# Batch 1's strided attention outputs: transposed by DMA through DRAM in place of TensorE

## The chip, the cores and the metric

The kernel runs on one core of one Trainium2 chip. The metric is device time in microseconds (us) of one execution, as a median over runs. Engines: PE is TensorE, DVE VectorE, ACT ScalarE, POOL GpSimd, SP SyncE, which only issues DMAs here. PEld in a profile is TensorE's weight loads, which overlap its matmuls.

## The reference

Sparse attention over 8 batches and 8 heads (576 positions, head size 64), then a bilinear feed-forward over all 4608 tokens:

```python
scores = scale * np.matmul(q, k.transpose(0, 1, 3, 2))
rel = pos[:, None] - pos[None, :]
mask_local = (rel >= 0) & (rel < stride)                 # stride 32
mask_strided = (rel >= 0) & (pos[None, :] % stride == pos[:, None] % stride)
masks = np.stack([mask_local if h < H // 2 else mask_strided for h in range(H)], axis=0)
...
attn_out = np.matmul(attn, v)                            # [8, 8, 576, 64]
x = attn_out.transpose(0, 2, 1, 3).reshape(B * S, H * D) # [4608, 512]
a = x @ w_a                                              # w_a, w_b: [512, 1536]
b = x @ w_b
return a * b @ w_out                                     # w_out: [1536, 512]
```

## The kernel before

**Tiling.** Attention is worked batch by batch, eight heads as four head pairs c = 0 to 3 (0 and 1 local, 2 and 3 strided) of two units each: u = 2c + half. The feed-forward is worked in nine tiles t of 512 tokens. Its input is `xT`, the attention output with features on the partitions and tokens along the row, one chunk of 128 features for each head pair; it is a ring of four batches (XR = 4). Batch 1 lies in columns 576 to 1151, of which tile 1 (tokens 512 to 1023) reads 576 to 1023 in all four chunks.

**An order written by hand.** All engines run their instructions in program order, which a table of slots sets. A tile has sixteen slots: twelve of `ffn_ab` (the products with w_a and w_b, L622) and four of `ffn_y` (the product with w_out, L872). Tile 0 is slots 0 to 15, tile 1 begins at slot 16. Positions such as 12.5 lie inside a slot. `STEPS[1]` (L580 to 582) lists what of batch 1's attention is issued at each position: T transposes q or k (`Tk`, `Tq`), S computes scores, exp and mask, V multiplies by the values and normalizes, X transposes a head pair's output into `xT`; L0 and L1 (`lead_vl`, L231) copy rows of `vl`, the local heads' values, on DVE; W0 to W3 (L175) make sums of `wo_sb`; D1 is the first step of batch 2's k. Slot 13 holds some(1) of six w_out matmuls, then position 12.5, three matmuls of each of the two token groups with 12.6 and 12.75 behind them, the last three of each, and position 13. The w_out matmuls at 6 to 8 and 9 to 11 of the second index read slices 2 and 3 of `wo_sb`, each loaded by its own DMA (L255).

**Outputs of batch 1.** V writes a normalized unit into `xn[1, z]` (a tile `xr`) with positions on the partitions; for the strided pairs (z = 1) that is 72 partitions by 8 positions by 4 heads by 64, position 8p + g on partition p. V5 completes pair 2, V7 completes pair 3. `step_X` (L564) then makes, for c >= 2, eight PE transposes of 72 by 128 into a `tp` bank (L550) and one ACT copy of 128 by 576 into `xT` (L562). X2 stands at position 12.75, X3 at 13, X0 at 14, X1 at 15.

**Values of batch 1.** V0, at position 13, is the first local unit of batch 1. It reads `vl_buf[1]`, which a GpSimd DMA loads (L225, issued behind the four DMAs of `wo_sb`), and whose first 32 partitions L0 copies from the others once the load has landed.

**The path through DRAM.** From batch 2 on the local pairs go another way: `rows_out` (O) writes a pair's outputs to a DRAM tile `xd`, as 576 rows of 128 numbers (144 KB), and `rows_in` (I) reads it back with a DMA transpose into `xT`. Both are issued on SP's queue in program order; the second waits on SP for the first to land. In `LATER` these are O0, I0, O1, and I1. Batches 0 and 1 do not use this path before the change.

**What tile 1 waits for.** At the first slot of tile 1 `ffn_ab` takes the chunks in the order 0, 2, 3 for w_a, then for w_b, and chunk 1 last (`late = 1`, L637), since X1 is the last step before.

**Loads.** GpSimd's queue issues all loads, with a conversion from float32 to bfloat16; in slots 0 and 1 the four `wo_sb` DMAs, `vl` of batch 1, and batch 2's k and q (L212, L203). SP's queue carries the results (L883 for tiles 0 and 1), batch 2's spread of k and q (L342, L346) and, from batch 2 on, O and I.

Of the kernel before, what the change touches and what calls it, by code (L numbers as in the profile page):

```python
# [17 lines left out]
NP = 72  # L18
# [3 lines left out]
LW = 96  # L22
# [9 lines left out]
def kernel(  # L32
# [10 lines left out]
    nc = tc.nc  # L43
    B, H, S, D = q.shape
# [392 lines left out]
    xn = {}  # L437
# [64 lines left out]
    scratch = {}  # L502

    def rows_out(b, c):

        scratch[b, c] = dram.tile([S, 2 * D], BF16, tag=f"xd{c}", name=f"xd{c}")
        nc.sync.dma_start(out=scratch[b, c].rearrange("(g p) (h d) -> p g h d", p=LW, d=D),
                          in_=xn[b, 0][:, :, 2 * c:2 * c + 2])

    def rows_in(b, c):  # L510

# [52 lines left out]
    def step_X(b, c):  # L564
# [12 lines left out]
        F1b F0c F1c""".split()  # L577


    STEPS = {1: {5.5: "Tk2", 6: "Tq2", 7: "S4 Tk3", 7.5: "S5", 8: "Tq3", 8.5: "V4", 9: "S6 V5 Pk0", 9.5: "S7 Pq0",  # L580
                 10: "V6 Tk0", 10.5: "Tq0 Pk1 Z0", 11: "Pq1", 12: "V7 Tk1 S0 W0 W1", 12.5: "Tq1 W2",
                 12.6: "S1", 12.75: "L0 X2", 13: "s2 X3 V0 m2 L1 W3", 13.5: "V1 S3", 14: "V2 X0", 14.5: "V3 D1", 15: "X1"},
             2: {20: "S0", 20.5: "S1", 21.5: "V0", 22: "S2", 23: "V1", 23.5: "S3", 24.5: "V2", 25: "S4", 26: "V3", 26.5: "S5",
                 27.5: "V4", 28: "S6", 28.5: "V5", 29: "S7", 29.5: "V6", 30.5: "V7"}}
    LATER = {-1: "S0", 0: "S1", 1: "V0", 2: "S2", 3: "V1 O0", 4: "S3", 5: "V2", 6: "S4 I0", 7: "V3 O1", 8: "S5", 9: "V4",
# [2 lines left out]
    IN_Y = {2: "S7", 6: "V6", 11: "V7"}  # L588
    FN = {"Tk": step_Tk, "Tq": step_Tq, "S": step_S, "V": step_V, "X": step_X, "W": lambda b, n: fast_w(n, slice(0, 3)),
          "s": S_px, "m": S_m, "L": lead_vl, "O": rows_out, "I": rows_in, "Pk": lambda b, c: pair_up("k", c), "Pq": lambda b, c: pair_up("q", c),  # L590
          "Z": lambda b, n: zero_qz(0, nc.vector, ((1, 1),)), "D": lambda b, n: step_D(FIRST_D, 0, "k", n)}

# [308 lines left out]
    with tc.manual_schedule(engines={ENG.PE, ENG.SP, ENG.Pool, ENG.DVE, ENG.Activation}):  # L901
# [11 lines left out]
        for x, src in ((raw[0], k), (raw[1], q)):  # L913
            nc.sync.dma_start(out=x[:96].rearrange("p (h r d) -> p h r d", h=2, d=D),
                              in_=src[0, 0:2].rearrange("h (p r) d -> p h r d", r=RL))
# [62 lines left out]
        for b in range(1, B):  # L978
            for pos, names in (STEPS.get(b) or {16 * (b - 1) + x: n for x, n in LATER.items()}).items():
                steps.setdefault(pos, []).append((b, names.split()))  # L980
            if b not in STEPS:
                for n, names in IN_Y.items():
# [104 lines left out]
```

## Time and profile before

| | us |
|---|---|
| median of 3 runs (lowest to highest) | 326.13 (326.02 to 326.52) |
| the profiled execution: its time | 326.3 |
| the profiled execution: its span in the trace | 324.6 |
| PE busy | 317.0 (98%) |
| DVE busy | 258.5 (80%) |
| ACT busy | 188.9 (58%) |
| POOL busy | 160.3 (49%) |
| packets of GpSimd's queue q0, share of 16 DMA engines over the span | 65.1% |
| packets of SP's queue q1, the same share | 25.3% |

The span runs from the first instruction to the last; 1.7 us of the profiled execution's time lie outside it. A busy share is a mean over stages: that PE is busy 98% of the span says that work taken from PE, or a wait put on it, shows in the time, if nothing else holds PE at that place. The DMA share can be above 100%, since packets of one engine overlap. The granted clock was 0.998 of full speed.

### The profile page before, as it was taken

How to read it: one execution, taken by the hardware profiler on the slowest of the kernel's cores; microseconds unless marked ns; L12 is line 12 of the kernel's file. 1: busy time of each engine (PE TensorE's matmuls, PEld its weight loads, DVE VectorE, ACT ScalarE, POOL GpSimd, SP SyncE). 2: the span in 40 equal slices, each digit the busy share in tenths (PEclk: the TensorE clock that was granted, in tenths of full speed). 3: DMA queues.
4: the chain of work that ended last, by engine and by line, in shares of the span. 5: the costliest groups of instructions: out<-in, count | busy, mean ns of one | idle time of the engine just before them, and what ended most of it. 6: DMA issues, size and time to landing. Idle time of an engine off the chain costs nothing.

```text
span 324.6 us, 7425 instructions
## 1 busy us (share of the span) xinstructions
PE 317.0 (98%) x2651; PEld 209.4 (65%) x2680; DVE 258.5 (80%) x559; ACT 188.9 (58%) x329; POOL 160.3 (49%) x289
## 2 busy tenths in 40 slices
PE   8999999999999999999999999999999999999994
PEld 7754555455555587557999885569455966686573
DVE  6767888888778899898889888988999768837842
ACT  6763775478764576447644764476546655335441
POOL 8945837699857554853576247644013012203300
PEclk9999999999999999999999999999999999999999
DMA  9999999899999999999999979999145040004004
GB/s 154 154 204 201 203 185 174 170 181 132 139 213 136 133 95 98 118 218 131 107 107 191 172 90 108 174 174 120 43 108 140 14 129 3 0 0 131 0 3 129
DMA packets 110724, 40.43 MB, mean 125 GB/s; under 512 B 88672, under 2 KB 107744, under 8 KB 110688
## 3 DMA queue, kind: packets, MB, share of 16 engines
q0 software_dynamic: 85968, 19.48, 65.1%
q1 hardware_dynamic: 24576, 20.42, 25.3%
q8 instruction: 21, 0.34, 0.5%
q14 instruction: 15, 0.12, 0.1%
q10 hardware_dynamic: 144, 0.07, 0.1%
HBM read 39.51 MB, written 10.91 MB: 155 GB/s over the span
## 4 chain that ended last, share of the span: by engine, by line
PE 88%; DMA 6%; POOL 2%; ACT 1%; DVE 1%; issue 1%; POOLq 0%
PE mm L622 46%; PE mm L808 14%; PE mm L872 6%; PE st L388 4%; PE mm L706 4%; PE o L466 2%; PE ax L699 2%; DMA xd<-xl 2%; PE o L525 2%; DMA xT<-xd 2%; DMA vl<-in_v_dram 2%; PE mm L699 2%; PE mm L837 2%; POOL shared L197 1%; PE end L837 1%; PE ab L622 1%
## 5 line engine op out<-in xcount | busy, mean ns | idle before, releaser
L622 PE MATMUL mm<-xT,wb_sb 128*128 128x512 bf16 (+1 forms) x404 | 93.3, 354 | 0.4
L622 PE MATMUL mm<-xT,wa_sb 128*128 128x512 bf16 (+1 forms) x391 | 92.1, 353 | 1.0 <-DMA xT<-xd 0.2
L643 ACT COPY a_sb<-mm 128x512 f32<-128x512 f32 x90 | 52.7, 586 | 53.8 <-PE mm L622 51.8
L622 PEld LDWEIGHTS <-wb_sb 128*128 128x128 bf16 x416 | 40.2, 98 | 36.6 <-DVE pf L711 0.4
L1053 POOL CAST pace<-pf 1x1 f32<-1x1 bf16 x83 | 24.9, 300 | 71.2 <-DVE pf L646 51.6
L646 DVE TENSOR_TENSOR pf<-a_sb,mm 128x512 bf16<-128x512 f32 x68 | 46.2, 680 | 9.6 <-PE mm L622 8.1
L622 PEld LDWEIGHTS <-wa_sb 128*128 128x128 bf16 x416 | 37.5, 98 | 24.4 <-issue 0.5
L409 ACT ACTIVATE p<-st 72x576 bf16<-72x576 f32 (+1 forms) x56 | 36.4, 650 | 14.4 <-PE st L388 14.2
L541 DVE TENSOR_TENSOR xT<-o,xr 64x288 bf16<-64x288 f32 x48 | 21.4, 446 | 14.8 <-ACT xr L535 14.3
L808 PEld LDWEIGHTS <-ps 128*128 128x128 bf16 x288 | 28.0, 98 | 3.1
L785 ACT COPY y_sb<-mm 128x512 f32<-128x512 f32 (+1 forms) x28 | 15.6, 556 | 17.9 <-PE mm L808 15.3
L808 PE MATMUL mm<-wf,ps 128*128 128x256 bf16 x216 | 25.5, 273 | 0.0
L534 ACT ACTIVATE xr<-o 64x576 f32<-64x576 f32 x28 | 18.1, 648 | 11.9 <-PE o L525 11.6
L872 PE MATMUL mm<-wo_sb,pf 128*128 128x512 bf16 x93 | 23.0, 379 | 0.2
L243 POOL DMA_DIRECT2D vs<-in_v_dram x24 | 19.6, 820 | 4.9 <-PE mm L808 2.4
L808 PEld LDWEIGHTS <-pf 128*128 128x128 bf16 x216 | 20.3, 98 | 2.6 <-issue 0.2
L1053 POOL COPY pace<-y_sb 1x1 f32<-1x1 f32 x23 | 5.2, 226 | 33.1 <-DVE y_sb L783 19.8
L535 ACT ACTIVATE xr<-xr 64x576 f32<-64x576 f32 x28 | 19.1, 683 | 0.9
L212 POOL DMA_DIRECT2D ql<-in_q_dram x24 | 16.0, 666 | 5.8 <-DMA wo_sb<-in_moe_w_out_dram 4.9
L808 PE MATMUL mm<-wo_sb,pf 128*128 128x256 bf16 x144 | 18.5, 273 | 0.1
L212 POOL DMA_DIRECT2D kl<-in_k_dram x24 | 16.1, 670 | 4.7 <-issue 3.9
L706 PE MATMUL mm<-xT,wb_sb 128*128 128x512 bf16 x60 | 18.3, 379 | 0.1
(189 smaller groups left out, 566.6 us busy)
## 6 DMA issues: line engine op xcount, KB each, us to landing
out_dram<-y_sb SPq DMA_DIRECT2D x12, 512.0 KB, 6.0
out_dram<-y_sb SPq DMA_DIRECT2D x11, 256.0 KB, 4.0
vl<-in_v_dram POOLq DMA_DIRECT2D x6, 384.0 KB, 8.2
kl<-in_k_dram POOLq DMA_DIRECT2D x24, 72.0 KB, 3.2
ql<-in_q_dram POOLq DMA_DIRECT2D x24, 72.0 KB, 3.4
vs<-in_v_dram POOLq DMA_DIRECT2D x24, 72.0 KB, 4.3
wo_sb<-in_moe_w_out_dram POOLq DMA_DIRECT2D x4, 384.0 KB, 9.7
natk<-in_k_dram POOLq DMA_DIRECT2D x20, 72.0 KB, 3.6
```

Source lines behind the costliest of these rows:

```text
L212: nc.gpsimd.dma_start(out=t[32 * h:32 * h + 32], in_=src[b, h].rearrange("(i y) d -> y i d", y=32))
L243: nc.gpsimd.dma_start(out=vs_buf[b % 2][:, h, :, 0:D], in_=v[b, HL + h].rearrange("(p r) d -> p r d", r=RS))
L409: nc.scalar.activation(p_flat(p)[:M, :2 * W].rearrange("p (i n) -> p i n", n=2 * n), st[:M].rearrange("p a (i n) -> p (a i) n", n=256)[:, ...
L535: nc.scalar.activation(r, r, ACT.Exp, scale=-1.0)
L541: nc.vector.tensor_mul(dst.rearrange("d (p r) -> d p r", r=RS)[:, :, G * half:G * (half + 1)], o[:64, j, :W].rearrange("d (g p) -> d p g", ...
L622: nc.tensor.matmul(ps_[:, c0:c0 + n], lhsT=w[:, kk, 128 * f:128 * (f + 1)], rhs=xT[:, kk, x0:x0 + n], start=(kk == first and c0 == 0), sto ...
L643: nc.scalar.copy(a_sb, ab[0])
L646: nc.vector.tensor_mul(pf[:, f, :].rearrange("p (i a s) -> p a i s", i=2, s=16), halves(a_sb), halves(ab[1]))
L706: nc.tensor.matmul(got[e], lhsT=wb_sb[:, kk, 128 * f:128 * (f + 1)], rhs=xT[:, kk, x0:x0 + TTOK], start=kk == 0, stop=kk == KD - 1)
L808: nc.tensor.matmul(bank[b][:, q], lhsT=lhs(g, q), rhs=rhs(g), start=k in "172" and q == 0 and g == 0, stop=g == FG - 1, skip_group_check=True)
L872: nc.tensor.matmul(ybank[j], lhsT=pf[:, f, 128 * j:128 * (j + 1)], rhs=wo_sb[:, f], start=(f == 0), stop=(f == FD - 1))
L1053: nc.gpsimd.tensor_copy(pace, done)
```

## The change

`rows_out` takes the strided pairs too: the DRAM tile's rows are then written as `(p g)`, 72 partitions by 8 rows, from `xn[b, 1]`. In the table of batch 1 the steps X2 (at 12.75) and X3 (at 13) go, and O2 comes behind V5 at slot 9, I2 behind V6 and Tk0 at slot 10, O3 behind V7 at slot 12, and I3 at 12.5 behind Tq1 and W2. X0 and X1 stay as they are. `rows_in` is unchanged.

```diff
     def rows_out(b, c):
 
         scratch[b, c] = dram.tile([S, 2 * D], BF16, tag=f"xd{c}", name=f"xd{c}")
-        nc.sync.dma_start(out=scratch[b, c].rearrange("(g p) (h d) -> p g h d", p=LW, d=D),
-                          in_=xn[b, 0][:, :, 2 * c:2 * c + 2])
+        order = dict(pattern="(g p) (h d) -> p g h d", p=LW) if c < 2 else dict(pattern="(p g) (h d) -> p g h d", p=NP)
+        nc.sync.dma_start(out=scratch[b, c].rearrange(order.pop("pattern"), d=D, **order),
+                          in_=xn[b, c // 2][:, :, 2 * (c % 2):2 * (c % 2) + 2])
...
-    STEPS = {1: {5.5: "Tk2", 6: "Tq2", 7: "S4 Tk3", 7.5: "S5", 8: "Tq3", 8.5: "V4", 9: "S6 V5 Pk0", 9.5: "S7 Pq0",
-                 10: "V6 Tk0", 10.5: "Tq0 Pk1 Z0", 11: "Pq1", 12: "V7 Tk1 S0 W0 W1", 12.5: "Tq1 W2",
-                 12.6: "S1", 12.75: "L0 X2", 13: "s2 X3 V0 m2 L1 W3", 13.5: "V1 S3", 14: "V2 X0", 14.5: "V3 D1", 15: "X1"},
+    STEPS = {1: {5.5: "Tk2", 6: "Tq2", 7: "S4 Tk3", 7.5: "S5", 8: "Tq3", 8.5: "V4", 9: "S6 V5 Pk0 O2", 9.5: "S7 Pq0",
+                 10: "V6 Tk0 I2", 10.5: "Tq0 Pk1 Z0", 11: "Pq1", 12: "V7 O3 Tk1 S0 W0 W1", 12.5: "Tq1 W2 I3",
+                 12.6: "S1", 12.75: "L0", 13: "s2 V0 m2 L1 W3", 13.5: "V1 S3", 14: "V2 X0", 14.5: "V3 D1", 15: "X1"},
```

## The prediction

> **What bounds the kernel now.** I read the page first (busy times), then TensorE's timeline around the two steps that go, then the timelines of VectorE and SyncE and the DMA issues of the same stretch, and last every DMA of the path through DRAM in the later batches.
>
> ```profile
> PE 317.0 (98%) x2651; PEld 209.4 (65%) x2680; DVE 258.5 (80%) x559; ACT 188.9 (58%) x329; POOL 160.3 (49%) x289
> ```
>
> PE is busy 98% of the span, so the whole kernel is bound by it; 16 transposes less should show, unless PE is held at this place by something else. TensorE's timeline there (start us, us, engine, line, what):
>
> ```profile
> 48.08 0.42 PE L550 MATMUL tp<-ident,xr 72*128 72x72 bf16 x8
> 48.34 1.46 PE L872 MATMUL mm<-wo_sb,pf 128*128 128x512 bf16 x5
> 49.64 0.41 PE L388 MATMUL st<-qz1l,kT1l 128*128 128x192 bf16 x3
> 49.89 0.42 PE L550 MATMUL tp<-ident,xr 72*128 72x72 bf16 x8
> 50.15 0.35 PE L466 MATMUL o<-vl,p 128*128 128x65 bf16 x6
> ...
> 56.87 0.81 PE L622 MATMUL mm<-xT,wa_sb 128*128 128x512 bf16 x3
> ```
>
> X2 starts at 48.08 and the next group at 48.34; X3 at 49.89, the next (V0) at 50.15. Each step takes 0.26 us of PE's order. Tile 1 begins at 56.87. What V0 needs is in VectorE's timeline, whose bracket gives the idle time before the row and what ended it, and in the DMA issues of 36.9 to 37 (KB and us to landing at the end):
>
> ```profile
> 49.73 0.35 DVE L231 COPY vl<-vl 32x704 bf16<-32x704 bf16 x1 [0.55 <-DMA vl<-in_v_dram]
> ```
>
> ```profile
> wo_sb<-in_moe_w_out_dram POOLq DMA_DIRECT2D x1, 384.0 KB, 11.9
> vl<-in_v_dram POOLq DMA_DIRECT2D x1, 288.0 KB, 12.8
> ```
>
> The load of `vl`, issued at 36.91, lands at 49.71. VectorE is waiting for it and copies until 50.08; V0 starts at 50.15. So V0 stands within 0.07 us of its data: X2 and X3 fill time that PE would otherwise wait. The loads before it are as tight: slice 3 of `wo_sb`, issued at 36.16, lands at 48.1, and the first matmul that reads it is in the row at 48.34. How full the DMA engines are is in the last two columns of the windows (DMA share, GB/s; the first is the stretch in us):
>
> ```profile
> 38.00:42.00 4.00, 4.00 (x48) 2.44 (x46) 3.78 (x11) 2.40 (x4) 2.69 (x5) 1.00 1.25 206
> 42.00:46.00 4.00, 3.94 (x37) 2.29 (x36) 3.43 (x9) 2.92 (x5) 0.82 (x2) 1.00 1.44 197
> 46.00:50.00 4.00, 3.95 (x38) 2.39 (x37) 2.68 (x6) 3.29 (x7) 1.33 (x3) 1.00 2.29 152
> 50.00:54.00 4.00, 4.00 (x48) 2.40 (x47) 3.32 (x10) 2.61 (x5) 4.00 (x8) 1.00 1.44 207
> ```
>
> Until 50 all of this is GpSimd's loads, with a share far over 1: they queue, and the landings above are 11.9 and 12.8 us after issue. PE is the bound by its busy time, but from 46 to 50 it walks just behind that queue.
>
> **What is removed.** Sixteen transposes, 2 x 0.26 = 0.52 us of PE, and two copies of 0.64 us on ACT. The copies lie off the path: ACT idles 0.75 us before the exp at 52.26. Without X2 and X3 PE comes to V0 at 50.15 - 0.52 = 49.63, but the copy of `vl` still ends at 50.08. Of the gain 50.15 - 50.08 = 0.07 us could be left; I take **0**. Behind V0 nothing changes for PE up to tile 1, and it shows no gap there to refill.
>
> **What is added, on SP.** SP's queue is empty from 15 to 49.80 (its first row there is the result store), so nothing holds O2. V5's last VectorE row is 0.69 us at 39.62: O2 issues at 40.4. The later batches show these operations so (SP's rows of 210 to 222, then of 242 to 256):
>
> ```profile
> L507 SPq DMA_DIRECT2D xd<-xl x1: 523/523/523, 215.5 to 215.5; - x1
> L512 SPq DMA_TRANSPOSE xT<-xd x2: 1148/1210/1271, 214.1 to 222.0; - x2
> DMA to landing us min/median/max: 6.1/6.5/7.0
> ```
>
> ```profile
> L507 SPq DMA_DIRECT2D xd<-xl x1: 534/534/534, 247.6 to 247.6; - x1
> L512 SPq DMA_TRANSPOSE xT<-xd x2: 1129/1142/1156, 246.3 to 250.0; - x2
> DMA to landing us min/median/max: 2.4/2.5/2.6
> ```
>
> With loads in flight (210 to 222, share 1.34) 6.1 to 7.0 us each, with none (246 on) 2.4 to 2.6. O2 alone in SP's queue beside loads is nearest to the write at 105.0, 3.4 us at a share of 0.9; at 1.25 to 1.44 I take 5.0 (bounds 3.4 and 6.5): it lands at 45.4. I2 issues then. O3 is queued behind it, and its data (VectorE's row of 0.69 us at 45.30) is there at 46.0. From the issue of a first transpose to the landing of the second, with a write queued between, the trace has 145.45 to 152.47 + 3.7 = 10.7 us, 179.88 to 190.5 = 10.7, 214.08 to 222.0 + 6.1 = 14.0 and, without loads, 246.35 to 252.6 = 6.2. With 10.7, I3 lands at **56.1**; at best O3 issues at 46.1 and I3 lands two transfers of 2.5 later, 51.1; at worst 46.9 + 14.0 = 60.9.
>
> PE wants I3's chunk as the third matmul of tile 1, 0.43 us into it: 57.30 now. So the middle case is in time. Behind I3 on SP wait the two stores of 49.80 and 50.45, whose buffer is needed again only in tile 1's `ffn_y` at 80 us, and batch 2's k at 57.07, behind I3's issue in every case but the last. No cost.
>
> **What is added, on the DMA engines.** Each of the four transfers moves 144 KB (147,456 bytes) on the engines that carry the loads. If the total rate stays, a transfer of SP's queue pushes the loads behind it by 147,456 bytes over the rate of the stretch: 0.72 us at 206 GB/s (O2, 41 to 45) and 0.97 us at 152 GB/s (I2, 45 to 50). Both are through before `vl`: **0.72 + 0.97 = 1.69 us later**, and O3 may add 0.97. The bounds: 0, if the loads keep their pace (50 to 54 moved 207 GB/s with the stores between, so 152 may not be a ceiling), and 2.66 with O3. I take 1.69, the two transfers that surely lie ahead of it. `wo_sb`'s slice 3 is late by part of the same, which is inside that and not added.
>
> The Trainium skill ("DMA: Bandwidth & Descriptors", section Queues, rings and completion order) says that each DMA engine alternates between the queues that have work, a whole packet at a time. By it the four transfers would not wait for the whole queue of loads, only share with it, and I3 would land near the early bound; the 256 KB store at 49.80, landed in 4.0 us while loads of 5 to 12 us were in flight, agrees. The sum stays 1.69, since by the rule the loads pay.
>
> A page that speaks against the change is "VectorE: DVE Perf Modes" (the Trainium skill, section Rules for kernel authors): transpose on TensorE where PSUM can take the result. The rows here, 0.26 us and a copy of 0.64 against two landings of 2.4 to 7.0, agree; it gives no other sum.
>
> **The sum.** V0 starts at 50.15 + 1.69 = 51.84, tile 1 at 58.56, and I3 (56.1) is there before 58.99. All behind moves with PE: with 98% busy no later gap takes 1.7 us back, and the loads after tile 0 are paced by GpSimd's copies of finished results. 326.3 + 1.69 - 0 = 328.0 for the profiled execution, which stands 0.17 above the median: **327.8**. By the bounds 0 and 2.66 it is 326.1 to 328.8.
>
> **Rivals.**
>
> *The transposed chunk comes late.* I3's landing takes the place of V0 as what holds PE, at the first slot of tile 1, from the point where it lands after 57.30 plus the loads' delay. At the slow bound 60.9 tile 1's third matmul is 3.6 us later than now: 329.7. For it: the share of 1.44 to 2.29 here is above that of the 14.0 us case. Against it: those landings had more of SP's own transfers between.
>
> *The loads keep their pace.* The engines take the 590 KB beside the loads, V0 stays pinned at 50.15, and nothing shows: 326.1. For it: the rate rose to 207 GB/s when stores came; against it: landings of 12 us show a queue that is full for 15 us.
>
> *Faster: V0 is not pinned.* The mechanism is at V0 too: it needs `vl` 0.5 us earlier than now. It decides if the load, bound by the order of packets and not by the engines, lands before 49.2; then the 0.52 us come through, 325.6, and with the two pauses before positions 42.3 and 48.8 in the chain of waits (0.06 and 0.05) 325.5. For it: `vl`'s landing is one execution's; against it: no edit hastens GpSimd's queue.
>
> **How the numbers follow.** My forecast gets 0.52, the late chunk 0.17, the loads at pace 0.18, V0 free 0.13. The predicted time is the first's, 327.8, its own range 326.8 (one transfer of 0.72) to 328.8. A measurement of this kernel can tell 0.2%, 0.65 us. Slower by more: the first and second, 0.69. Within: the third and some 0.05 of the fourth, 0.23. Faster by more: what is left of the fourth, 0.08, as its full 0.63 us just meets the bound. The range has to take in all but 0.2: from 325.8 (half of the gain) to 329.8 (the late chunk at its bound).
>
> **What would show it.** L550 with 40 transposes for 56, L562 with 6 copies; four more SP rows with `xd`. Right, if VectorE's row of L231 stands near 51.4 with a wait on `vl`, V0 near 51.8 and tile 1 near 58.6 with no wait on `xT`. The late chunk would show as a wait of L622 on the DMA `xT<-xd` near 58 to 61. The loads at pace: L231 at 49.7 still. Wrong altogether, if V0 starts before 50.0.

## The result and the profile after

The changed kernel takes 331.35 us (median of 5 runs, 331.14 to 332.76) against 326.52 us of the kernel before beside it: a ratio of 1.0163 (of the means; 95% interval 1.014 to 1.0185), 4.8 us slower by the medians. Forecast was 327.8, in a range that ended at 329.8. The direction was right, the size was not, and the mechanism was that of the first rival. Here are busy times and granted clock of the page:

```profile
span 329.5 us, 7426 instructions
PE 320.7 (97%) x2664; PEld 209.7 (64%) x2664; DVE 259.0 (79%) x559; ACT 187.9 (57%) x327; POOL 160.5 (49%) x289
PEclk9999999799999999999999999999999999999998
```

TensorE does 16 transposes less, but the two busy times (317.0 before, 320.7 after) don't compare: the page before has 2651 matmuls for 2680 weight loads, so its trace lacks some records, and the page after has 2664 for 2664. The clock row is the sign to go by: ahead of the run's end one slice in 40 has a lower granted clock, the one from 57.7 to 65.9 us. That is where tile 1 begins. TensorE's timeline there:

```profile
50.90 0.31 PE L466 MATMUL o<-vl,p 128*128 128x65 bf16 x5 [0.19 <-DVE vl L231]
...
57.58 0.60 PE L623 MATMUL mm<-xT,wa_sb 128*128 128x512 bf16 x2
61.13 0.38 PE L623 MATMUL mm<-xT,wa_sb 128*128 128x512 bf16 x1 [2.96 <-DMA xT<-xd]
61.35 1.36 PE L623 MATMUL mm<-xT,wb_sb 128*128 128x512 bf16 x3
...
63.36 1.78 PE L623 MATMUL mm<-xT,wa_sb 128*128 128x512 bf16 x4
```

Two matmuls of tile 1 run, on chunks 0 and 2. The third needs chunk 3, and TensorE stands still for 2.96 us until I3 has landed. What follows runs slowly: four matmuls take 1.78 us at 63.36, where the same group took 1.03 us before:

```profile
58.59 1.03 PE L622 MATMUL mm<-xT,wa_sb 128*128 128x512 bf16 x4
```

The windows (stretch; busy us of PE, PEld, DVE, ACT, POOL; granted clock; DMA share; GB/s) show why:

```profile
60.00:61.00 1.00, 0.00 (x0) 0.00 (x0) 0.00 (x0) 0.00 (x0) 0.96 (x1) 1.00 1.09 394
61.00:62.00 1.00, 0.86 (x3) 0.34 (x3) 0.00 (x0) 0.00 (x0) 0.17 (x1) 0.73 1.07 393
62.00:63.00 1.00, 1.00 (x4) 0.36 (x3) 0.00 (x0) 0.00 (x0) 0.00 (x0) 0.50 0.66 234
63.00:64.00 1.00, 1.00 (x4) 0.38 (x3) 0.20 (x1) 0.59 (x1) 0.00 (x0) 0.50 0.35 102
64.00:65.00 1.00, 1.00 (x4) 0.32 (x3) 1.00 (x2) 0.00 (x0) 0.17 (x1) 0.56 0.33 77
65.00:66.00 1.00, 1.00 (x6) 0.46 (x5) 0.97 (x3) 0.59 (x1) 0.90 (x1) 1.00 0.43 110
```

After the wait the granted clock is 0.50 for some 3.4 us (by what the windows from 61 to 65 lack to 1.00). SyncE's queue shows why I3 is late:

```profile
40.95 1.02 SPq L508 DMA_DIRECT2D xd<-xr  x1
48.86 1.23 SPq L513 DMA_TRANSPOSE xT<-xd  x1
50.13 0.85 SPq L508 DMA_DIRECT2D xd<-xr  x1
55.06 1.13 SPq L513 DMA_TRANSPOSE xT<-xd  x1
```

O2 is issued at 40.95, and I2, which waits for it to land, at 48.86: **7.9 us** for a write that took 2.4 to 7.0 us in the later batches. O3, whose data is there at 46.6, is behind I2 and goes out at 50.13; I3 follows at 55.06 (4.9 us) and lands 6.03 us later, at 61.09.

The loss, as places in the two traces. Third matmul of tile 1: 57.30 before, 61.13 after, so 3.8 us, of which 0.7 us had been there at V0 (50.15 and 50.90). By 66 us the same rows stand 5.5 us apart: the half clock adds 1.7 us. From 228 us on 5.1 us are left, and the spans differ by 4.9. V0's own start is set by the copy of `vl`, in VectorE's timeline:

```profile
50.50 0.35 DVE L231 COPY vl<-vl 32x704 bf16<-32x704 bf16 x1 [0.54 <-DMA vl<-in_v_dram]
```

It stands 0.77 us later than before, where the prediction had about 1.69. TensorE was 0.8 us late at 44 us already, before O2 had moved a packet, so this lateness is the execution's own. The two steps that are gone would have left 0.3 us of it at V0; the wait for `vl`, which landed 13.3 us after its issue in place of 12.8, made it 0.7 again.

### The profile page after: what moved, and what is told of

Read it like the earlier page. It is cut to its first block, busy times and chain, and to the rows that moved or that the text cites. A ratio compares the mean times of both kernels' runs of the same rounds, so it can differ in the third digit from the quotient of the medians.

```text
span 329.5 us, 7426 instructions
## 1 busy us (share of the span) xinstructions
PE 320.7 (97%) x2664; PEld 209.7 (64%) x2664; DVE 259.0 (79%) x559; ACT 187.9 (57%) x327; POOL 160.5 (49%) x289
## 4 chain that ended last, share of the span: by engine, by line
PE 83%; DMA 11%; POOL 2%; DVE 1%; ACT 1%; issue 0%
PE mm L623 41%; PE mm L809 17%; DMA shared<-in_k_dram 4%; PE mm L707 4%; DMA vl<-in_v_dram 4%; PE st L388 4%; PE mm L873 3%; PE misc L155 3%; PE o L526 2%; PE ax L700 2%; DMA xT<-xd 2%; PE mm L838 2%; PE mm L700 2%; DMA xd<-xr 1%; PE o L466 1%; PE end L838 1%
## 5 line engine op out<-in xcount | busy, mean ns | idle before, releaser
L623 PE MATMUL mm<-xT,wa_sb 128*128 128x512 bf16 (+1 forms) x408 | 94.9, 357 | 3.0 <-DMA xT<-xd 3.0
L623 PE MATMUL mm<-xT,wb_sb 128*128 128x512 bf16 (+1 forms) x408 | 94.5, 356 | 0.2 <-DMA wb_sb<-in_moe_w_b_dram 0.2
L647 DVE TENSOR_TENSOR pf<-a_sb,mm 128x512 bf16<-128x512 f32 x68 | 46.3, 680 | 9.2 <-PE mm L623 8.1
L786 ACT COPY y_sb<-mm 128x512 f32<-128x512 f32 (+1 forms) x28 | 15.6, 556 | 17.8 <-PE mm L809 14.5
L535 ACT ACTIVATE xr<-o 64x576 f32<-64x576 f32 x28 | 18.1, 648 | 11.9 <-PE o L526 11.6
L649 DVE TENSOR_TENSOR pf<-a_sb,mm 128x512 bf16<-128x512 f32 x22 | 14.9, 677 | 8.5 <-ACT a_sb L644 6.6
L707 PE MATMUL mm<-xT,wb_sb 128*128 128x512 bf16 x64 | 19.0, 379 | 0.0
```

Of the source, the lines that this page charges most:

```text
L535: nc.scalar.activation(r, sums, ACT.Ln)
L623: nc.tensor.matmul(ps_[:, c0:c0 + n], lhsT=w[:, kk, 128 * f:128 * (f + 1)], rhs=xT[:, kk, x0:x0 + n], start=(kk == first and c0 == 0), sto ...
L647: nc.vector.tensor_mul(pf[:, f, :].rearrange("p (i a s) -> p a i s", i=2, s=16), halves(a_sb), halves(ab[1]))
L707: nc.tensor.matmul(got[e], lhsT=wb_sb[:, kk, 128 * f:128 * (f + 1)], rhs=xT[:, kk, x0:x0 + TTOK], start=kk == 0, stop=kk == KD - 1)
```

## The experiments

Theory *late chunk*: the four DMAs wait for each other on SyncE's queue, I3 comes after TensorE asks for it, and TensorE's idling lowers its clock. Rival *loads pay*: what the prediction took for the likeliest, the added bytes push `vl` and thereby V0 back.

### One pair through DRAM

```diff
-  12: "V7 O3 Tk1 S0 W0 W1", 12.5: "Tq1 W2 I3", ... 13: "s2 V0 m2 L1 W3"
+  12: "V7 Tk1 S0 W0 W1", 12.5: "Tq1 W2", ... 13: "s2 X3 V0 m2 L1 W3"
```

> Pair 2 alone goes through DRAM (O2, I2); pair 3 keeps its eight TensorE transposes (X3). Theory 'late chunk' (the four DMAs wait for each other in SyncE's queue, so that pair 3's chunk lands at 61.1 us, after TensorE asks for it at 58.2): I2 lands near 54.5 us, before tile 1's first slot at 57 to 58, TensorE waits for no xT<-xd there, keeps its clock, and the time is that of before, 326.1 to 326.8. Theory 'loads pay' (the added bytes push GpSimd's loads back): half of the added 5 us stays, 327.5 to 329.

Measured 326.48 us, ratio 0.9996 (0.9985 to 1.0007): the whole loss is gone. The profiled execution, TensorE's timeline:

```profile
58.43 0.81 PE L623 MATMUL mm<-xT,wa_sb 128*128 128x512 bf16 x3
```

Chunks 0, 2 and 3 follow each other with no wait; I2, issued at 49.68, had landed by 55.5. Late chunk holds. In this execution, the longest of the twelve, `vl` landed 14.5 us after its issue (12.8 before), so that V0 stood waiting until 51.75; how often that happens, and whether O2's bytes are the reason, isn't shown. No gain shows either, but X2's 0.26 us would be a ratio of 0.9992, which the interval takes in, so this run can't tell whether they come through.

### The traffic without its consumers

```diff
-  out=xT[:, c, S * (b % XR):S * (b % XR + 1)]
+  out=xT[:, c, S * ((b if b > 1 else 3) % XR):S * ((b if b > 1 else 3) % XR + 1)]
   # X2 and X3 stay; O2, I2, O3, I3 as in the change
```

> All four DMAs are added to the kernel before, but their result goes to columns of xT that batch 3 overwrites later; X2 and X3 stay on TensorE, so nothing of tile 1 waits for them. 'Late chunk': the traffic alone costs little, the copy of vl on VectorE moves by 0 to 0.5 us, time 326.1 to 327.0. 'Loads pay' as in the prediction: vl 1.69 us later, 327.8 to 328.4.

Measured 327.24 us, ratio 1.0012 (0.9996 to 1.0027): some 0.4 us, not told from none, just above the one expectation and well under the other. VectorE's timeline:

```profile
50.18 0.35 DVE L231 COPY vl<-vl 32x704 bf16<-32x704 bf16 x1 [0.71 <-DMA vl<-in_v_dram]
```

The copy starts 0.45 us later than before, where the prediction had 1.69. In the mean the traffic costs little. But the twelve runs fall into two halves: six from 325.84 to 326.79, of which the traced one is one, and six from 327.69 to 328.05, above all 29 runs of the kernel before beside them (at most 327.43). What made those longer wasn't traced, so a cost of over 1 us in some runs isn't ruled out.

### TensorE kept busy while it waits

```diff
+  for _ in range(14 if t == 1 and f == 0 and last < 0 and ps_ is ab[0] else 0):
+      nc.tensor.matmul(ps_, lhsT=w[:, 0, 128 * f:128 * (f + 1)], rhs=xT[:, 0, TTOK * t:TTOK * (t + 1)],
+                       start=True, stop=True)
```

> The changed kernel with 14 repeated matmuls of 128x512 (each 0.216 us) on TensorE between chunks 0, 2 and 3 of tile 1's first slot, where it waits 2.96 us; their sums are overwritten. If the halved granted clock from 61.3 to 64.6 us comes from TensorE's idling, the clock stays at 1.0 and the time falls by 1.5 to 1.8 us to 329.5 to 329.9. If the wait alone makes the loss, or the clock drops for another reason, the time stays at 331.3 or rises.

Measured 329.83 us, ratio 1.0092 (1.0076 to 1.0108) against 1.0163: 1.5 us by the medians, 2.3 us by the ratios, with work added. In TensorE's timeline the 14 stand ahead of chunk 0, not between the chunks:

```profile
57.17 3.19 PE L621 MATMUL mm<-xT,wa_sb 128*128 128x512 bf16 x14
60.19 0.59 PE L626 MATMUL mm<-xT,wa_sb 128*128 128x512 bf16 x2
61.72 0.38 PE L626 MATMUL mm<-xT,wa_sb 128*128 128x512 bf16 x1 [0.93 <-DMA xT<-xd]
61.93 0.81 PE L626 MATMUL mm<-xT,wb_sb 128*128 128x512 bf16 x3
```

I3 is no earlier (61.67), but the matmuls behind it take 0.81 us for three, where the changed kernel had 1.36, and the granted clock is 1.00 in every window from 56 to 66. It is the idling that halves the clock, and this is the price of that part of the loss.

### Neither transposes nor DMAs

```diff
-  9: "S6 V5 Pk0 O2", 10: "V6 Tk0 I2", 12: "V7 O3 Tk1 S0 W0 W1", 12.5: "Tq1 W2 I3"
+  9: "S6 V5 Pk0", 10: "V6 Tk0", 12: "V7 Tk1 S0 W0 W1", 12.5: "Tq1 W2"
+  do(3, lambda: nc.vector.memset(xT[:, 2:4, S:2 * S], 0.0))
```

> X2 and X3 go and nothing takes their place: batch 1's strided outputs are left out (their part of xT is set to zero by one VectorE memset at slot 3). If V0 is pinned by the load of vl, as the prediction has it, V0 starts where it did (50.1 us) and the time stays at 326.0 to 326.5. If the 0.52 us of TensorE's time come through, V0 starts near 49.6 us and the time is 325.5 to 325.9.

Measured 327.11 us, ratio 1.0007 (0.9994 to 1.002). Above both expectations in us, but no gain against the kernel before beside it (326.6). VectorE's timeline:

```profile
49.95 0.38 DVE L231 COPY vl<-vl 32x704 bf16<-32x704 bf16 x1
```

The copy ends at 50.33 and V0 starts at 50.36. But the row has no bracket: `vl` was issued at 36.72 and landed 12.5 us later, at 49.22, so here `vl` did not hold V0. TensorE came to this stage 0.73 us later than in the trace of before and was 0.21 us later at V0: the whole 0.52 us came through and made up lateness. The memset (0.54 us on VectorE at 27.37) cost TensorE nothing; the distance to the trace of before is 0.62 us from 14 to 36 us. At the end TensorE is through 0.14 us sooner than before, and the span is longer all the same, since the last 64 KB store takes 3.7 us to land, where it took 2.5 before. So the time shows no gain, but this run doesn't show that `vl` is the reason, and whether the 0.52 us can be had stays open.

### Where a write waits

Writes of O2's shape that nobody waits for were added to the kernel before:

```diff
+  def probe(n, src, parts=(slice(0, NP),)):
+      t = dram.tile([S, 2 * D], BF16, tag=f"pr{n}", name=f"pr{n}")
+      for p in parts:
+          nc.sync.dma_start(out=t.rearrange("(p g) d -> p g d", p=NP)[p], in_=src()[p])
   ...
+  for n, i in enumerate((3, 6, 9)):
+      do(i, probe, n, two(0))
+  do(12, probe, 3, two(1))
   ...
```

> The kernel before, with writes of the kind of O2 (72 partitions by 8 rows of 256 bytes, 144 KB) to unused DRAM tiles, nobody waiting for them: at slots 3, 6 and 9 (about 25, 30 and 36 us, while the loads in flight move pieces of 1 KB), at slot 12 (about 46 us, pieces of 128 bytes), and near 256 us, where no load is in flight; there once more, split into 64 and 8 partitions. If a queue of loads in large pieces holds SyncE's packets back, the first three land 7 to 9 us after issue with their first packet 3 to 5 us behind it, the fourth in 4 to 5.5 us, and the last in about 2.5 us. If the shape (72 partitions) makes the write slow, the one near 256 us lands late too (over 4 us) and the split one sooner. If any full queue does it, the fourth is as late as the first three. Time: 326 to 328.5.

SyncE did not wait for the slots: it issued the first three from 17.84 us on and the fourth at 43.32. So the test of the fourth at 46 us failed, and the time (two runs, median 328.65, ratio 1.0066, 1.0044 to 1.0088, over the expected bound) has more traffic at an earlier place in it. What the DMA queues moved from 18 to 22 us (packets, MB, share of 16 engines; q0 is GpSimd's, q1 SyncE's):

```profile
q0 software_dynamic: 1037, 0.80, 129.3%
```

From 22 to 26:

```profile
q0 software_dynamic: 683, 0.68, 101.0%
q1 hardware_dynamic: 439, 0.11, 21.0%
```

For 4 us after the first issue SyncE's queue moves nothing. Then it gets two packets of 256 bytes for every three of GpSimd's, a seventh of the bytes, and the three writes need 14.5 us, 22.1 to 36.6. The loads slow down too, from 0.80 to 0.68 MB in 4 us, and TensorE is 2.9 us late at 40 us against the trace of before. With no load in flight the writes near 255 moved from 255.5 to 257.2. These two came from a tile whose rows merge into pieces of 2 KB (180 packets for 0.30 MB), so they are no test of the shape; a short queue, below, is one. They were through 2.6 us after the first issue. The fourth write met the `wo_sb` loads that were late by then: issued at 43.32, it moved its first packet at 47.4 and its last at 51.6.

### Small pieces first

Loads in pieces of 1 KB (`wo_sb`) might hold SyncE's packets longer than those of 128 bytes (`vl`, k, q):

```diff
-  for c in range(4):
-      do(0, load_wo, c)
+  do(0, load_wo, 0)
   do(0, load_vl, 1)
+  do(0, load_qk, FIRST_D, False)
+  for c in range(1, 4):
+      do(0, load_wo, c)
```

> The changed kernel with GpSimd's loads in another order: only the first slice of wo_sb, then vl and batch 2's first k and q (pieces of 128 bytes), then the other three slices (pieces of 1 KB). O2 then meets small pieces from about 41 us on. If loads in large pieces are what delays SyncE's first packet by 4 us, that packet comes 1 to 2.5 us after O2's issue and O2 lands in 4 to 6 us in place of 7.9. If any full queue of loads does it, the packet comes after 4 us again and O2 lands after 7 to 8 us. The late slices of wo_sb hold TensorE, so the time is no test of it: 330 to 340.

335.39 us (one run). SyncE's queue:

```profile
40.02 1.02 SPq L508 DMA_DIRECT2D xd<-xr  x1
47.88 1.33 SPq L513 DMA_TRANSPOSE xT<-xd  x1
```

7.9 us again, and SyncE's queue moved its first packet at 43.8, 3.8 us after the issue. The piece size is not the cause: that guess falls, and "any full queue of loads" stands. The late slices of `wo_sb` kept TensorE waiting for 7.67 us, up to 51.11, and its clock fell here too: 0.55 from 46 to 50 us, 0.50 from 50 to 54.

### A short queue of loads

```diff
-  out=wo_sb[:, 3 * c:3 * (c + 1)], in_=...[:, 3 * c:3 * (c + 1)]
+  out=wo_sb[:, 3 * c:3 * (c + 1), :64], in_=...[:, 3 * c:3 * (c + 1), :64]
+  do(2, lambda: nc.vector.memset(wo_sb[:, :, 64:], 0.0))
```

> The changed kernel with wo_sb's four loads cut to 64 of 512 columns; the other columns are left out (set to zero by one VectorE memset at slot 2), so the queue of loads that O2 meets at 41 us is short, while every other DMA stays. If the backlog of GpSimd's queue is what delays O2, vl lands well before 12 us after issue, O2's first packet comes within 2 us, O2 lands in 2.5 to 5 us, I3 lands by 56 us, TensorE waits for no xT<-xd at tile 1, the clock stays full, V0 is no longer held by vl, and the time is 324.8 to 326.8. If the delay belongs to the write itself, O2 lands after 7 to 8 us again and the time stays near 331.

SyncE's queue and then TensorE's timeline:

```profile
40.91 1.02 SPq L508 DMA_DIRECT2D xd<-xr  x1
45.60 1.22 SPq L513 DMA_TRANSPOSE xT<-xd  x1
46.88 0.85 SPq L508 DMA_DIRECT2D xd<-xr  x1
53.32 1.13 SPq L513 DMA_TRANSPOSE xT<-xd  x1
```

```profile
56.97 0.81 PE L623 MATMUL mm<-xT,wa_sb 128*128 128x512 bf16 x3
```

`vl` lands 5.8 us after issue in place of 13.3, O2 in 4.7 in place of 7.9 with its first packet after 2.0 us, I3 at 55.8; no wait, and the clock is 1.00. The write's shape is the same, so the backlog is what delays O2. O3 still took 6.4 us, with I2's packets between. The time missed its expectation, at 328.11 us, ratio 1.0043 (1.0021 to 1.0065): in the profiled execution (326.51) TensorE falls back by 0.6 us at 28 us, against the trace of before, right behind the added memset (2.30 us on VectorE from 25.69); 0.52 of it are back at V0 (50.21), which waits for nothing. The last 64 KB store lands after 3.4 us in place of 2.5. The other runs are longer, and why was not followed further.

### Other orders

Both writes ahead of both transposes on SyncE:

```diff
-  10: "V6 Tk0 I2", ... 12: "V7 O3 Tk1 S0 W0 W1"
+  10: "V6 Tk0", ... 12: "V7 O3 I2 Tk1 S0 W0 W1"
```

> The changed kernel with SyncE's order O2 O3 I2 I3 in place of O2 I2 O3 I3: O3 no longer waits behind I2 for O2's landing. If the four landings one after the other make the chunk late, O3 is issued near 46.8 us, I3 near 50 to 52 and lands at 56 to 58 us, TensorE waits at most 0.5 us in tile 1's first slot, keeps its clock, and the time falls to 326.3 to 327.5. If the DMA engines' capacity sets the landing of the last one, I3 still lands after 60 us and the time stays at 330 to 331.5.

Measured 328.26 us, ratio 1.0076 (1.0046 to 1.0107), between the two. TensorE's timeline:

```profile
59.67 0.38 PE L623 MATMUL mm<-xT,wa_sb 128*128 128x512 bf16 x1 [1.53 <-DMA xT<-xd]
```

I3 lands at 59.63, 1.5 us sooner, not 3 to 5: O3 goes out at 46.90, but lands only when I3 is issued, at 54.28. So the order costs 1.5 us of the lateness, and the rest is the transfers' own. The profiled execution's clock is 1.00. Two of the eight runs have a mean clock of 0.993 and take 330.6 and 331.8 us, the others 0.997 to 1.0 and 327.6 to 328.5. How long TensorE waited in those two was not traced.

Chunk 3 last in tile 1's first slot:

```diff
-  late = 1 if t == 1 else 3
+  late = 3
```

> The changed kernel with chunk 3 taken last in tile 1's first slot in place of chunk 1: TensorE asks for it four matmuls later (0.86 us). It waits up to 0.8 us for X1's copy first, and then for I3. If a long idle time is what halves the clock, two short waits cost less: 328.0 to 330. If the sum is only shifted and the clock drops just the same, 330.3 to 331.3.

Measured 329.14 us, ratio 1.0095 (1.0067 to 1.0124), inside the first expectation. TensorE's timeline:

```profile
58.65 0.59 PE L623 MATMUL mm<-xT,wa_sb 128*128 128x512 bf16 x2 [0.74 <-ACT xT L563]
...
61.11 0.38 PE L623 MATMUL mm<-xT,wa_sb 128*128 128x512 bf16 x1 [1.22 <-DMA xT<-xd]
```

The waits sum to 1.96 us in two pieces, I3 is as late as ever (61.06), and the clock stays full in this execution; in two of six runs it is 0.993 to 0.994, at 330.9 and 331.4 us.

Both edits together:

> SyncE's order O2 O3 I2 I3 and chunk 3 taken last in tile 1's first slot, the two edits that each took 2 to 3 us off the changed kernel. If only I3's landing (59.6 us with the first edit) stands against TensorE's asking (58.4 us plus the wait for X1's copy of 0.7 us, so 59.1), the wait on it is 0 to 0.6 us, the clock stays full, and the time is 326.8 to 327.8, still no gain over the kernel before. If the pair-3 path could be hidden and the 0.52 us of TensorE came through, 325.8 to 326.2.

Measured 327.75 us, ratio 1.0041 (1.0025 to 1.0057). The wait on I3 is 0.71 us, a little over the bound. No order that was tried beats the kernel before, and leaving the two steps out altogether showed no gain in the time either.

## Why the prediction was wrong

**Right.** That the 0.52 us of TensorE show no gain: without X2 and X3 the ratio is 1.0007, and the interval leaves out the 0.9984 that they would make, though a longer last store is in that ratio too. The reason given, V0 pinned by `vl`, fits the trace of before (V0 0.07 us behind the copy) and that of the changed kernel (V0 waits 0.19 us for the copy). In the trace without X2 and X3 it doesn't hold: there the 0.52 us came through up to V0. The changed kernel is slower, and the rival *the transposed chunk comes late* named the wait, its place (the third matmul of tile 1) and the chain that makes it; its slow bound for I3, 60.9, is 0.2 us from the measured 61.09. That closeness is luck: O2 landed 2.0 us behind its slow bound (48.86 against 46.9), and the rest of the chain took 1.8 us less than its own (12.2 against 14.0).

**The step that failed** is O2's landing: "O2 alone in SP's queue beside loads is nearest to the write at 105.0, 3.4 us at a share of 0.9; at 1.25 to 1.44 I take 5.0 (bounds 3.4 and 6.5): it lands at 45.4". It took 7.9 us, outside the bounds, and landed at 48.86. The row was chosen because O2 stands alone on SyncE's queue, and its time was raised for the DMA share. But seven of the ten writes of the later batches took 5.3 to 7.0 us, and at 105 the loads were paced and landed 3.5 us after issue; those in flight at 41 landed 11.9 and 12.8 us after issue, as the prediction's own rows show. With the queue thinned O2 landed in 4.7 us. From there the prediction's chain ran nearly as written: 48.86 plus 12.2 us from I2's issue to I3's landing (10.7 taken, 14.0 as the bound) gives 61.1. So 3.5 of the 5.0 us that I3 was later than forecast are O2's (2.9 its length, 0.55 its later issue), 1.5 the rest's.

**The term that was missing** is the clock. The rival was priced at 329.7, by the wait alone. The wait was 2.96 us, and the halved clock behind it cost 1.7 us more in the trace; with TensorE kept busy, the ratio fell from 1.0163 to 1.0092. 329.7 and 1.7 make 331.4, close to the measured 331.35; that they meet so well is chance, since the wait was shorter than the 3.6 us of the rival, TensorE came late to it, and 0.4 us come back near 228 us.

**The term that was too large** is the loads' delay, 1.69 us. The traffic alone cost 0.45 us at the copy of `vl` in the trace, and 0.1% of the time in the mean of its runs, half of which were longer than any of before. In the changed kernel I2, for which 0.97 of the 1.69 us were set down, moved its first packet at 51.3, when `vl` had landed (50.4), so that part fell out: O2's lateness that made the chunk late also kept I2 away from the loads. The two terms were taken as independent, and here they are not.

**Two rules against the runs.** By the Trainium skill ("DMA: Bandwidth & Descriptors", section Queues, rings and completion order) the engines alternate between queues; from that the prediction had I3 land near the early bound. The packets that did flow, 439 against 683, look like alternation, though not by equal bytes (0.11 against 0.68 MB). But nothing in that reading gives the 4 us in which SyncE's queue moved nothing; the measurement decides, and the store at 49.80 that was called its witness had met loads that landed some 5 us after issue, not 12. The rule that would have priced the clock is in "TensorE: Matmul & The Clock Gate" (the Trainium skill, Part 1: The HAM clock gate): after an idle window of some 3.4 us the array runs at half its clock, until it has been busy for as long. The trace agrees on the half clock and on how long it lasts, some 3.4 us at 0.50; but a wait of 2.96 us was enough for it here.

## What to carry to other kernels

A transfer's latency beside a backlog was not to be read here from the share of busy engines, but from how long the other transfers in flight took to land: where they took 12 us, a small write on another queue took 8, and the chain of four transfers took 20 us (40.95 to 61.09). A wait on TensorE is priced with the clock that it loses: near 3 us of idling cost another 1.7 us here. The profiled executions with waits of 0.7 to 1.5 us kept the full clock. And before an engine's time is counted as gained, find which load holds its next instruction: here 0.52 us of the bounding engine never showed in the time.

## What was not expected of the hardware

Beside a full queue of GpSimd's loads, the first packet of a DMA issued on SyncE came about 4 us after its issue (40.95 to 45.2, 17.84 to 22.1, 43.32 to 47.4; 40.02 to 43.8 with the loads in pieces of 128 bytes). It hardly varied: O2 took 4.2 to 4.3 us to its first packet in the runs with one pair, with the traffic alone, with TensorE kept busy and with both writes first as well. With the queue thinned it was 2.0 us, and in the kernel before, among the paced loads of batch 3, 1.1 us (105.0 to 106.1). Then the 576 packets of O2 took 3.2 us in the changed kernel, and 2.3 with the thinned queue. What the 4 us consist of is open.
